# Two layers of a dense network on one core: fewer, larger weight loads, and x transposed in halves

## The chip, the cores and the metric

The kernel runs on one core of a Trainium2 chip. The metric is the device time of one execution in microseconds (us), taken over repeated runs. A profile of one execution gives a span (from the first to the last instruction), which is a little shorter than the device time.

## The reference

The kernel computes a dense layer with a GELU, and a second dense layer, for 512 rows (16 x 32) of 1024 features, with 3584 hidden features; everything is bf16.

```python
B, S, D, F = 16, 32, 1024, 3584
def reference(x, w1, b1, w2, b2):
    h = jnp.einsum("bsd,df->bsf", x, w1) + b1
    h = _gelu(h)
    return jnp.einsum("bsf,fd->bsd", h, w2) + b2
```

x is 1 MB, w1 and w2 are 7 MB each, the output is 1 MB. Each layer is 224 matmuls of 128 x 128 weights against 512 columns.

## The kernel before, in words

Everything is kept in on-chip memory, with a tile of its own for each load (pool `const`), so that no load waits for a buffer. All loads are issued by SyncE (`nc.sync`) in the order in which they are written: the four row tiles of x (`x_sb0` to `x_sb3`, line 60), eight chunks of w1 for its first 512 columns, one for each block `dt` of 128 input features (`w1a`, line 66, 128 KB each), with `b1_rows` (line 70) after the first of them, six chunks of 512 columns over all of `dt` (`w1c`, line 74, 1 MB each), fourteen chunks of w2 (`w2c`, line 83, 512 KB each), and b2. The names in the profile carry a buffer number: w1c_90 is the first 1 MB chunk. A scheduler adds the semaphores; it gives the loads eight semaphores in turn, so that a load is issued only once the load eight places before it has landed.

TensorE first runs `NWARM` = 5 matmuls on zeros (line 99). Then it transposes x: for each row tile, eight 128 x 128 transposes into one PSUM tile (line 109), of which VectorE copies the first half (dt 0 to 3, line 110) and ScalarE the second half (dt 4 to 7, line 111) into `xT`. b1 is transposed and copied after that (lines 114 and 116).

Layer one runs first over a group of `FTC` = 4 output tiles of 128 hidden features together, with `dt` in the outer loop, so that matmuls can start when the first chunk of w1 is there (line 126). Its four GELUs follow (ScalarE, line 121). The remaining 24 tiles run one after the other, each with its eight `dt` matmuls (line 140) and a GELU into `hT`. Layer two runs over two halves of the output columns and four row tiles, with 28 matmuls each (line 154); VectorE adds b2 (line 162) and SyncE stores.

All PSUM tiles come from one pool of eight banks in rotation: the ninth tile waits until the first has been read.

Of the kernel before, what the change touches and what calls it, by code (L numbers as in the profile page):

```python
# [1 line left out]

# [5 lines left out]

ACT = mybir.ActivationFunctionType
ALU = mybir.AluOpType  # L10
FP32 = mybir.dt.float32
BF16 = mybir.dt.bfloat16
PSUM = bass.MemoryType.PSUM

NWARM = 5


@with_exitstack
def kernel(
    ctx: ExitStack,  # L20
    tc: tile.TileContext,
    x: bass.AP,
    w1: bass.AP,
    b1: bass.AP,
    w2: bass.AP,
    b2: bass.AP,
    out: bass.AP,
):
    nc = tc.nc
    P = 128  # L30

    xf = x.flatten_outer_dims()
    of = out.flatten_outer_dims()
    N, D = xf.shape
    F = w1.shape[1]
    assert N % P == 0 and D % P == 0 and F % P == 0
    NT, DT, FT = N // P, D // P, F // P
    assert N <= 512
    FC = 512
    FTC = FC // P  # L40
    assert F % FC == 0
    NFC = F // FC
    DC = 512
    assert D % DC == 0
    NDC = D // DC

    const = ctx.enter_context(tc.tile_pool(name="const", bufs=1))
    opool = ctx.enter_context(tc.tile_pool(name="opool", bufs=3))
    psum = ctx.enter_context(tc.tile_pool(name="psum", bufs=8, space=PSUM))

    def ps_tile(shape, dtype):
        return psum.tile(shape, dtype, name="ps", tag="ps")

    w1v = w1.rearrange("(dt p) f -> p dt f", p=P)
    w2v = w2.rearrange("(ft p) d -> p ft d", p=P)

    x_sb = []
    for nt in range(NT):
        t = const.tile([P, D], BF16, name=f"x_sb{nt}")
        nc.sync.dma_start(t[:], xf[nt * P:(nt + 1) * P, :])  # L60
        x_sb.append(t)

    w1_first = []
    for dt in range(DT):
        t = const.tile([P, FC], BF16, name=f"w1a{dt}")
        nc.sync.dma_start(t[:], w1v[:, dt, 0:FC])  # L66
        w1_first.append(t)
        if dt == 0:
            b1_rows = const.tile([FT, P], BF16, name="b1_rows")
            nc.sync.dma_start(b1_rows[:], b1.rearrange("(ft p) -> ft p", p=P))  # L70
    w1_ch = [None]
    for c in range(1, NFC):
        t = const.tile([P, DT, FC], BF16, name=f"w1c{c}")
        nc.sync.dma_start(t[:], w1v[:, :, c * FC:(c + 1) * FC])
        w1_ch.append(t)

    W2FT = 4
    NW2 = FT // W2FT
    w2_ch = [[None] * NW2 for _ in range(NDC)]
    for dc in range(NDC):  # L80
        for c in range(NW2):
            t = const.tile([P, W2FT, DC], BF16, name=f"w2c{dc}_{c}")
            nc.sync.dma_start(t[:], w2v[:, c * W2FT:(c + 1) * W2FT, dc * DC:(dc + 1) * DC])
            w2_ch[dc][c] = t

    b2_sb = const.tile([P, D], BF16, name="b2_sb")
    nc.sync.dma_start(b2_sb[:], b2[None, :].to_broadcast((P, D)))

    warm = const.tile([P, 1], FP32, name="warm")
    nc.gpsimd.memset(warm[:], 0.0)  # L90
    warm2 = const.tile([P, 1], FP32, name="warm2")
    nc.scalar.activation(warm2[:], warm[:], ACT.Gelu_apprx_tanh)

    zeros = const.tile([P, 512], BF16, name="zeros")
    nc.vector.memset(zeros[:], 0.0)  # L95
    if NWARM:
        warm_ps = ps_tile([P, 512], FP32)
        for i in range(NWARM):
            nc.tensor.matmul(warm_ps[:], lhsT=zeros[:, 0:P], rhs=zeros[:], start=True, stop=True)  # L99

    ident = const.tile([P, P], BF16, name="ident")
    make_identity(nc, ident[:])

    xT = const.tile([P, DT, N], BF16, name="xT")
    H = DT // 2
    for nt in range(NT):
        tp = ps_tile([P, DT, P], BF16)
        for dt in range(DT):
            nc.tensor.transpose(tp[:, dt, :], x_sb[nt][:, dt * P:(dt + 1) * P], ident[:])  # L109
        nc.vector.tensor_copy(xT[:, 0:H, nt * P:(nt + 1) * P], tp[:, 0:H, :])  # L110
        nc.scalar.copy(xT[:, H:DT, nt * P:(nt + 1) * P], tp[:, H:DT, :])  # L111

    b1_ps = ps_tile([P, FT], BF16)
    nc.tensor.transpose(b1_ps[:], b1_rows[:], ident[:FT, :FT])
    b1_sb = const.tile([P, FT], FP32, name="b1_sb")
    nc.vector.tensor_copy(b1_sb[:], b1_ps[:])

    hT = [const.tile([P, N], BF16, name=f"hT{ft}") for ft in range(FT)]

    def gelu(ft, ps):  # L120
        nc.scalar.activation(hT[ft][:], ps[:], ACT.Gelu_apprx_tanh, bias=b1_sb[:, ft:ft + 1], scale=1.0)  # L121

    ps_first = [ps_tile([P, N], FP32) for _ in range(FTC)]
    for dt in range(DT):
        for j in range(FTC):
            nc.tensor.matmul(  # L126
                ps_first[j][:],
                lhsT=w1_first[dt][:, j * P:(j + 1) * P],
                rhs=xT[:, dt, :],
                start=(dt == 0),  # L130
                stop=(dt == DT - 1),
            )
    for j in range(FTC):
        gelu(j, ps_first[j])

    for ft in range(FTC, FT):
        c, j = divmod(ft, FTC)
        ps = ps_tile([P, N], FP32)
        for dt in range(DT):
            nc.tensor.matmul(  # L140
                ps[:],
                lhsT=w1_ch[c][:, dt, j * P:(j + 1) * P],
                rhs=xT[:, dt, :],
                start=(dt == 0),
                stop=(dt == DT - 1),
            )
        gelu(ft, ps)

    for dc in range(NDC):
        for nt in range(NT):  # L150
            ps = ps_tile([P, DC], FP32)
            for ft in range(FT):
                c, j = divmod(ft, W2FT)
                nc.tensor.matmul(  # L154
                    ps[:],
                    lhsT=hT[ft][:, nt * P:(nt + 1) * P],
                    rhs=w2_ch[dc][c][:, j, :],
                    start=(ft == 0),
                    stop=(ft == FT - 1),
                )  # L160
            o_sb = opool.tile([P, DC], BF16, name="o_sb")
            nc.vector.tensor_tensor(o_sb[:], ps[:], b2_sb[:, dc * DC:(dc + 1) * DC], ALU.add)  # L162
            nc.sync.dma_start(of[nt * P:(nt + 1) * P, dc * DC:(dc + 1) * DC], o_sb[:])


# [1 line left out]
_INS = ['x', 'w1', 'b1', 'w2', 'b2']  # L167
_OUTS = [((16, 32, 1024), 'bfloat16')]


# [23 lines left out]
```

## Time and profile before

| what | value |
|---|---|
| device time, median of 6 runs | 110.06 us (109.81 to 111.14) |
| span of the profiled execution | 108.8 us |
| TensorE matmul, busy | 102.1 us (94%), 486 instructions |
| ScalarE / VectorE, busy | 22.7 us / 7.6 us |
| DMA: moved, mean rate | 17.11 MB, 157 GB/s over the span |
| DMA queue of SyncE | 49.0% of 16 engines' span |

Busy time of TensorE is the sum of stretches in which a matmul was under way; matmuls overlap in their pipeline, so their rate is better read from the distance of their starts. A wait is put down to the event that came last before the waiting instruction started. The profile's page also divides the span into 40 slices of 2.72 us, with a digit for the busy share of each engine.

### The profile page before, as it was taken

How to read it: one execution, taken by the hardware profiler on the slowest of the kernel's cores; microseconds unless marked ns; L12 is line 12 of the kernel's file. 1: busy time of each engine (PE TensorE's matmuls, PEld its weight loads, DVE VectorE, ACT ScalarE, POOL GpSimd, SP SyncE). 2: the span in 40 equal slices, each digit the busy share in tenths (PEclk: the TensorE clock that was granted, in tenths of full speed). 3: DMA queues.
4: the chain of work that ended last, by engine and by line, in shares of the span. 5: the costliest groups of instructions: out<-in, count | busy, mean ns of one | idle time of the engine just before them, and what ended most of it. 6: DMA issues, size and time to landing. Idle time of an engine off the chain costs nothing.

```text
span 108.8 us, 1129 instructions
## 1 busy us (share of the span) xinstructions
PE 102.1 (94%) x486; PEld 46.6 (43%) x486; DVE 7.6 (7%) x14; ACT 22.7 (21%) x34; POOL 0.7 (1%) x7
## 2 busy tenths in 40 slices
PE   5869979999999999999999999999999999999970
PEld 2444424444444444444444444444444444444420
DVE  0330000000000000000000020202011020202020
ACT  5160083534435243342522000000000000000000
POOL 2000000000000000000000000000000000000000
PEclk9999999999999999999999999999999999999999
DMA  3998999999999999994000010010101010100101
GB/s 75 277 327 271 366 351 348 352 316 356 333 285 322 364 350 349 351 347 148 4 0 0 0 48 0 5 49 0 48 0 48 0 48 0 44 4 6 48 0 48
DMA packets 16702, 17.11 MB, mean 157 GB/s; under 512 B 698, under 2 KB 16058, under 8 KB 16698
## 3 DMA queue, kind: packets, MB, share of 16 engines
q1 hardware_dynamic: 16698, 17.05, 49.0%
q8 instruction: 4, 0.07, 0.3%
HBM read 16.00 MB, written 1.05 MB: 157 GB/s over the span
## 4 chain that ended last, share of the span: by engine, by line
PE 83%; DMA 11%; SPq 2%; DVE 1%; issue 0%
PE ps L154 44%; PE ps L140 38%; DMA w1c_90<-in_w_dram 7%; DMA w1a_72<-in_w_dram 4%; SPq L60 2%; DVE o_sb L162 1%; SPq L66 0%
## 5 line engine op out<-in xcount | busy, mean ns | idle before, releaser
L162 DVE TENSOR_TENSOR o_sb<-ps,b_sb 128x512 bf16<-128x512 f32 x8 | 5.5, 692 | 92.8 <-PE ps L154 92.8
L140 PE MATMUL ps<-xT,w1c_90 128*128 128x512 bf16 x32 | 7.1, 379 | 0.7 <-DMA w1c_90<-in_w_dram 0.7
L140 PE MATMUL ps<-xT,w1c_92 128*128 128x512 bf16 x32 | 7.1, 379 | 0.0
L140 PE MATMUL ps<-xT,w1c_94 128*128 128x512 bf16 x32 | 7.1, 379 | 0.0
L140 PE MATMUL ps<-xT,w1c_96 128*128 128x512 bf16 x32 | 7.1, 379 | 0.0
L140 PE MATMUL ps<-xT,w1c_98 128*128 128x512 bf16 x32 | 7.1, 379 | 0.0
L140 PE MATMUL ps<-xT,w1c_100 128*128 128x512 bf16 x32 | 7.1, 379 | 0.0
L140 PEld LDWEIGHTS <-w1c_90 128*128 128x128 bf16 x32 | 3.1, 98 | 4.7 <-DMA w1c_90<-in_w_dram 1.1
L140 PEld LDWEIGHTS <-w1c_98 128*128 128x128 bf16 x32 | 3.1, 98 | 3.8
L140 PEld LDWEIGHTS <-w1c_100 128*128 128x128 bf16 x32 | 3.1, 98 | 3.8
L140 PEld LDWEIGHTS <-w1c_96 128*128 128x128 bf16 x32 | 3.1, 98 | 3.8
L140 PEld LDWEIGHTS <-w1c_94 128*128 128x128 bf16 x32 | 3.1, 97 | 3.8
L140 PEld LDWEIGHTS <-w1c_92 128*128 128x128 bf16 x32 | 3.1, 97 | 3.8
L99 PE MATMUL ps<-zeros 128*128 128x512 bf16 x5 | 2.3, 626 | 1.2 <-DVE zeros L95 1.2
L111 ACT COPY xT<-ps 128x512 bf16<-128x512 bf16 x4 | 2.2, 588 | 3.8 <-DVE xT L110 3.8
L110 DVE COPY xT<-ps 128x512 bf16<-128x512 bf16 x4 | 1.7, 425 | 4.8 <-PE ps L109 4.8
L121 ACT ACTIVATE hT_198<-ps,b_sb 128x512 bf16<-128x512 f32 x1 | 0.7, 687 | 5.9 <-PE ps L126 5.9
L154 PE MATMUL ps<-w2c_0_102,hT_198 128*128 128x512 bf16 x4 | 1.5, 379 | 0.0
L154 PE MATMUL ps<-w2c_0_102,hT_199 128*128 128x512 bf16 x4 | 1.5, 379 | 0.0
L154 PE MATMUL ps<-w2c_0_102,hT_200 128*128 128x512 bf16 x4 | 1.5, 379 | 0.0
L154 PE MATMUL ps<-w2c_0_102,hT_201 128*128 128x512 bf16 x4 | 1.5, 379 | 0.0
L154 PE MATMUL ps<-w2c_1_104,hT_202 128*128 128x512 bf16 x4 | 1.5, 379 | 0.0
(144 smaller groups left out, 138.0 us busy)
## 6 DMA issues: line engine op xcount, KB each, us to landing
w1c_90<-in_w_dram SPq DMA_DIRECT2D x1, 1024.0 KB
w1c_92<-in_w_dram SPq DMA_DIRECT2D x1, 1024.0 KB, 10.5
w1c_94<-in_w_dram SPq DMA_DIRECT2D x1, 1024.0 KB, 14.5
w1c_96<-in_w_dram SPq DMA_DIRECT2D x1, 1024.0 KB, 13.1
w1c_98<-in_w_dram SPq DMA_DIRECT2D x1, 1024.0 KB, 13.3
w1c_100<-in_w_dram SPq DMA_DIRECT2D x1, 1024.0 KB, 13.0
out_dram<-o_sb SPq DMA_DIRECT2D x8, 128.0 KB, 1.7
w2c_0_102<-in_w_dram SPq DMA_DIRECT2D x1, 512.0 KB, 9.9
```

The source lines that it names most:

```text
L60: nc.sync.dma_start(t[:], xf[nt * P:(nt + 1) * P, :])
L99: nc.tensor.matmul(warm_ps[:], lhsT=zeros[:, 0:P], rhs=zeros[:], start=True, stop=True)
L110: nc.vector.tensor_copy(xT[:, 0:H, nt * P:(nt + 1) * P], tp[:, 0:H, :])
L111: nc.scalar.copy(xT[:, H:DT, nt * P:(nt + 1) * P], tp[:, H:DT, :])
L121: nc.scalar.activation(hT[ft][:], ps[:], ACT.Gelu_apprx_tanh, bias=b1_sb[:, ft:ft + 1], scale=1.0)
L140: nc.tensor.matmul(ps[:], lhsT=w1_ch[c][:, dt, j * P:(j + 1) * P], rhs=xT[:, dt, :], start=(dt == 0), stop=(dt == DT - 1),)
L154: nc.tensor.matmul(ps[:], lhsT=hT[ft][:, nt * P:(nt + 1) * P], rhs=w2_ch[dc][c][:, j, :], start=(ft == 0), stop=(ft == FT - 1),)
L162: nc.vector.tensor_tensor(o_sb[:], ps[:], b2_sb[:, dc * DC:(dc + 1) * DC], ALU.add)
```

## The change

The change is meant to let layer one start earlier and to have fewer, larger loads. It has these parts:

- The row tiles x1 and x3, and then `b1_rows`, are issued by ScalarE's queue; x0 and x2 by SyncE.
- The first group of layer one has `G0` = 8 tiles of hidden features in place of 4. Its w1 chunks are 128 x 1024 (256 KB); that of dt 0 comes in two halves. Its GELUs are written directly after the last matmul of each tile.
- The rest of w1 comes in two chunks of 1024 columns (2 MB each: w1c8 and w1c16) and one of 512 (w1c24).
- w2 comes in seven chunks of whole rows (1 MB each) in place of fourteen of half rows.
- The warm-up is 22 matmuls of 128 columns in place of 5 of 512.
- x is transposed in half tiles (dt 0 to 3, and dt 4 to 7), each in a PSUM tile of its own: x0 and x1 whole, then b1, then the first halves of x2 and x3, then their second halves. The copies of x2 and x3 are split between the two engines so that the first halves are copied side by side.

```diff
-NWARM = 5
+NWARM = 22
...
-        nc.sync.dma_start(t[:], xf[nt * P:(nt + 1) * P, :])
+        (nc.sync if nt % 2 == 0 else nc.scalar).dma_start(t[:], xf[nt * P:(nt + 1) * P, :])
...
+    b1_rows = const.tile([FT, P], BF16, name="b1_rows")
+    nc.scalar.dma_start(b1_rows[:], b1.rearrange("(ft p) -> ft p", p=P))
...
+    HC = G0C // 2
+    w1p0 = []
+    for h in range(2):
+        t = const.tile([P, HC], BF16, name=f"w1p0_{h}")
+        nc.sync.dma_start(t[:], w1v[:, 0, h * HC:(h + 1) * HC])
+        w1p0.append(t)
+    w1p = [None]
+    for dt in range(1, DT):
+        t = const.tile([P, G0C], BF16, name=f"w1p{dt}")
+        nc.sync.dma_start(t[:], w1v[:, dt, 0:G0C])
+        w1p.append(t)
...
+    while f0 < FT:
+        n = min(8, FT - f0)
+        t = const.tile([P, DT, n * P], BF16, name=f"w1c{f0}")
+        nc.sync.dma_start(t[:], w1v[:, :, f0 * P:(f0 + n) * P])
+        w1_chunks.append((f0, n, t))
+        f0 += n
...
+    for c in range(NW2):
+        t = const.tile([P, W2FT, D], BF16, name=f"w2c{c}")
+        nc.sync.dma_start(t[:], w2v[:, c * W2FT:(c + 1) * W2FT, :])
+        w2_ch.append(t)
...
-            nc.tensor.matmul(warm_ps[:], lhsT=zeros[:, 0:P], rhs=zeros[:], start=True, stop=True)
+            nc.tensor.matmul(warm_ps[:], lhsT=zeros[:], rhs=zeros[:], start=True, stop=True)
...
+    for nt in (0, 1):
+        a = transpose_half(nt, 0)
+        b = transpose_half(nt, 1)
+        copy_half(nt, 0, a, "v")
+        copy_half(nt, 1, b, "s")
+    b1_sb = const.tile([P, FT], FP32, name="b1_sb")
     b1_ps = ps_tile([P, FT], BF16)
     nc.tensor.transpose(b1_ps[:], b1_rows[:], ident[:FT, :FT])
-    b1_sb = const.tile([P, FT], FP32, name="b1_sb")
     nc.vector.tensor_copy(b1_sb[:], b1_ps[:])
+
+    a2 = transpose_half(2, 0)
+    a3 = transpose_half(3, 0)
+    copy_half(2, 0, a2, "s")
+    copy_half(3, 0, a3, "v")
+    b2_ = transpose_half(2, 1)
+    b3_ = transpose_half(3, 1)
+    copy_half(2, 1, b2_, "v")
+    copy_half(3, 1, b3_, "s")
...
-    ps_first = [ps_tile([P, N], FP32) for _ in range(FTC)]
+    ps_first = [ps_tile([P, N], FP32) for _ in range(G0)]
     for dt in range(DT):
-        for j in range(FTC):
+        for j in range(G0):
...
+            if dt == DT - 1:
+                gelu(j, ps_first[j])
```

## The prediction

> **What bounds the kernel now.** I read the page first: TensorE (PE) is busy 94% of the span of 108.8 us, while the DMA engines are busy only in the first half.
>
> ```profile
> PE 102.1 (94%) x486; PEld 46.6 (43%) x486; DVE 7.6 (7%) x14; ACT 22.7 (21%) x34; POOL 0.7 (1%) x7
> ...
> PE   5869979999999999999999999999999999999970
> ...
> DMA  3998999999999999994000010010101010100101
> ```
>
> So the loads end near 50 us, and PE is gapped only in the first six slices and in the last. The chain of waits, in order of time, says the same.
>
> ```profile
> 7.36 7.99 DMA w1c_90<-in_w_dram
> 15.35 0.05 issue
> 15.39 41.61 PE ps L140 x192
> 57.01 48.36 PE ps L154 x224
> ```
>
> From 15.39 on PE runs without a hole, until the last add and store: 41.61 / 192 = 0.217 and 48.36 / 224 = 0.216 us for each matmul. Only what precedes 15.39 can shrink. The timeline of PE in the first 20 us shows that stretch (start, duration, engine, line; in brackets the idle time before it and what ended it).
>
> ```profile
> 1.19 2.31 PE L99 MATMUL ps<-zeros 128*128 128x512 bf16 x5 [1.19 <-DVE zeros L95]
> 3.46 1.00 PE L109 MATMUL ps<-ident,x_sb_64 128*128 128x128 bf16 x8
> ...
> 5.73 0.62 PE L109 MATMUL ps<-ident,x_sb_68 128*128 128x128 bf16 x8 [0.82 <-DMA x_sb_68<-in_x_dram]
> 6.54 0.62 PE L109 MATMUL ps<-ident,x_sb_70 128*128 128x128 bf16 x8 [0.18 <-DMA x_sb_70<-in_x_dram]
> 7.09 0.18 PE L114 MATMUL ps<-ident,b_rows 28*128 28x28 bf16 x1
> 7.67 1.02 PE L126 MATMUL ps<-xT,w1a_72 128*128 128x512 bf16 x4 [0.40 <-DVE xT L110]
> ...
> 13.71 1.03 PE L126 MATMUL ps<-xT,w1a_88 128*128 128x512 bf16 x4
> 15.39 4.92 PE L140 MATMUL ps<-xT,w1c_90 128*128 128x512 bf16 x22 [0.65 <-DMA w1c_90<-in_w_dram]
> ```
>
> There are two losses. The first real matmul starts at 7.67, after the fourth x tile lands (6.53), is transposed and copied. The first 32 matmuls should be over at 13.71 + 4 x 0.216 = 14.57, but the next group starts at 15.39, when w1c_90 has landed: a hole of 0.82 us. Next I read how fast the loads came, by stretches (stretch, length, PE, PEld, DVE, ACT, POOL busy, clock, DMA share, GB/s).
>
> ```profile
> 2.40:3.40 1.00, 1.00 (x3) 0.15 (x1) 0.00 (x0) 0.00 (x0) 0.00 (x0) 1.00 1.03 395
> 3.40:4.60 1.20, 1.20 (x15) 1.14 (x15) 0.10 (x1) 0.00 (x0) 0.00 (x0) 1.00 0.82 157
> 4.60:7.40 2.80, 1.67 (x23) 1.22 (x21) 1.38 (x4) 1.62 (x3) 0.00 (x0) 1.00 1.03 356
> 7.40:9.80 2.40, 2.13 (x10) 0.97 (x10) 0.32 (x2) 0.62 (x2) 0.00 (x0) 1.00 0.83 234
> 9.80:15.35 5.55, 4.94 (x23) 2.05 (x21) 0.00 (x0) 1.22 (x3) 0.00 (x0) 1.00 1.04 356
> 18.35:22.95 4.60, 4.60 (x23) 2.06 (x21) 0.00 (x0) 1.81 (x3) 0.00 (x0) 1.00 1.10 350
> ```
>
> The reader sees two dips: 157 GB/s at 3.4 to 4.6 us, with the engines still 0.82 busy (slow packets, cause not shown), and 234 GB/s at 7.4 to 9.8, where the engines were short of work. In the second, SyncE issues 128 KB chunks and each waits for the transfer eight places earlier to land (w1a_84 is issued at 5.70, x_sb_68 landed at 5.65; w1a_86 at 6.51, when x_sb_70 landed). It costs 2.4 x (350 - 234) = 0.28 MB, 0.8 us of streaming.
>
> **What the Trainium skill says.** "DMA: Bandwidth & Descriptors", section "Issuing engines are not separate DMA queues": issuing from a second engine saves only issue time, as all transfers run on the same 16 engines. In the trace an issue takes 0.42 to 0.43 us on SyncE, and the four x issues go from 0.74 to 2.54. The same page, "Queues, rings and completion order": completion isn't in order over the 16 engines. The trace agrees: w1c_90 is complete when 3.15 MB have been asked for up to its end, but the windows add up to some 4.2 MB moved by then, so the slowest engine lags the mean by about 1 MB. The same page, "Why small descriptors are slow (HBM only)": a packet has a fixed overhead. The trace agrees: 395 GB/s in 2.4 to 3.4 us, when x rows of 2 KB moved, against 350 with w1's 1 KB rows. "TensorE: Matmul & The Clock Gate", section "Part 1: The HAM clock gate": PE is at half clock until it has been busy for about 3.4 us, whatever the number of matmuls. Here matmuls start 0.43 us apart at 1.6 to 2.4 us and 0.216 apart from 7.67; transposes go from 0.10 apart (x_sb_64) to 0.057 (x_sb_66, 4.3 to 4.7), so the clock rose near 4.2, 3.0 us after PE's start.
>
> **The change part by part.**
> *x on two queues.* All x issues end by about 1.6 instead of 2.54, but the data share one set of engines. Earliest: 1.05 MB from 2.4 on at 395 GB/s without the first dip, 2.4 + 2.66 = 5.1, plus the 0.3 by which landing trails: 5.4. Latest: 6.5 as before, as the bytes ahead of the last x byte are the same. I take the middle, 5.95, for x2, x3 and b1_rows, which follows x3 on ScalarE's queue.
> *Transposes and copies in halves.* The b1 transpose now stands on PE ahead of x2 and x3, so all of them wait for b1_rows. After that: b1 0.1, a2 and a3 8 x 0.057 = 0.46, about 0.1 until the output can be read, then DVE's copy of a3, 0.42: 1.1 us to the first matmul. Before it was 7.67 - 6.53 = 1.14. So the interleaving wins next to nothing itself: it replaces four transposes by the b1 pair on the path. ScalarE's copy of a2 (0.59) begins 0.23 earlier than a3's copy and ends with it. The second halves of x2 and x3 are copied beside the first 32 matmuls, which read dt 0 to 3 alone; two of the first eight wait for these copies through the PSUM rotation, but 1.3 and 1.5 us after the first, and the copies are done by then. First matmul: 5.95 + 1.1 = 7.05; bounds 6.5 and 7.65. Win 0.6 (0 to 1.2).
> *ScalarE.* Three issues of about 0.43 go ahead of its table load (1.28) and warm activation (0.20): done at 0.74 + 1.3 + 1.5 = 3.5. Its first copy was at 4.96. Nothing.
> *Warm-up, 22 narrow matmuls for 5 wide.* At half clock 22 x 0.105 (the x_sb_64 spacing) = 2.3 us, against 2.31. Nothing, unless the clock rises later.
> *First group of 8 tiles, in 256 KB chunks.* The first group has 64 matmuls, 13.8 us, so the next chunk is due at 7.05 + 13.8 = 20.9. Each dt chunk lasts PE 8 x 0.216 = 1.73 us and takes 0.26 / 0.35 = 0.75 us to stream, so they keep up. The starvation of 7.4 to 9.8 goes, since twice the bytes are in flight behind the same eight places. Gelus now run as each tile of the group ends: eight in 4.7 us at the 0.58 spacing of before, starting 1.5 us before the group's end; the next PSUM tiles are wanted 1.73 us apart. Hidden.
> *The chunk w1c8.* It is 2 MB and ends at the position, 5.25 MB, at which w1c_94 ended; that landed at 22.95 (issued 8.46, 14.5 us). Less 0.8 for the starvation: 22.2 at the old pace. With 2 KB rows at 395/350 the stretch from about 6.6 shrinks from 15.6 to 13.8: 20.4. So 20.4 to 22.2 against a need at 20.9; I take the early end, since the 395 is in this trace. The hole of 0.82 is gone then.
> *w2 in whole rows.* All seven chunks are now wanted in the first 28 matmuls of layer two, 6 us from about 55 on, rather than over 48 us. Loads ended at 50 before, and don't end later. Hidden. Layer two and the tail keep their matmuls, adds and stores.
> Sum: 0.6 + 0.8 = 1.4 us; 110.06 - 1.4 = 108.7.
>
> **The rivals.** For all: before, the 65th matmul started at 15.39 + 32 x 0.217 = 22.3; the win is 22.3 less its new start.
> (a) *x lands when it did.* Start 7.65, next group at 21.5: 109.3. For: bytes ahead are equal, and the first dip may return. Against: x2 and x3 are asked for 0.5 to 0.9 us sooner.
> (b) *A new hole before w1c8.* The chunk lands at 21.5 to 22.2 and PE waits there, whatever the start: 109.3 to 110.0. For: w1c_94 at 22.95. Against: wider rows.
> (c) *Worse than that.* If the fast engines run ahead by as many packets as before, now of 2 KB, the lag goes from about 1.6 MB at w1c_94 to 3.2: at 395 GB/s (5.25 + 3.2 - 1.3) / 0.395 = 18.1 after 6.6: 24.7, and 112.5. Against: the lag grew with bytes moved, not at once.
> (d) *Cold clock.* If x0 and x1, now loaded side by side, both come near 4.1, PE idles 0.6 between warm-up and transposes, and one more half-clock stretch of 3.4 us may fall on the first 8 matmuls: 8 x 0.21 = 1.7, next group at 22.6, 110.4; two stretches, 112.1.
>
> **How the numbers follow.** The forecast (107.9 to 109.0 with the start's bounds) has 0.53, (a) 0.14, (b) 0.19, (c) 0.06, (d) 0.08. Range 107.9 to 110.5: it leaves out (c), half of (d) and a little below. Faster by over 1% means under 108.96: 0.54. Slower means over 111.16: 0.10. The rest, 0.36, is within.
>
> **What would show it.** Right: first w1p_0 matmul at 6.5 to 7.5; no idle time of PE, or under 0.3 us, put down to w1c8; over 370 GB/s from 8 to 20 us and no dip at 7.4 to 9.8; 0.216 us spacing from the first matmul. Wrong: a wait of over 0.5 us on w1c8 or on a w1p chunk, 0.43 us spacing in the first group, or PE held at the b1 transpose past 6.5.

## The result, and the profile after

| | before | changed |
|---|---|---|
| device time, median | 110.27 us (40 runs) | 109.44 us (20 runs) |
| ratio, changed to before | | 0.9934, 95% interval 0.9912 to 0.9957 |

The changed kernel is faster by 0.7% (0.4 to 0.9% by the interval): 0.83 us between the medians, where 1.36 us was forecast. The profile kept of it is of one of its longer executions (110.90 us), which the ratio leaves out, so a second profile is shown below with the experiments. First the page of the first profile: the busy time of TensorE, its busy tenths in 40 slices, and those of the DMA engines.

```profile
PE 104.1 (95%) x503; PEld 49.7 (46%) x503; DVE 7.5 (7%) x14; ACT 22.1 (20%) x34; POOL 0.7 (1%) x7
...
PE   6799999999999999999999999999999999999970
...
DMA  2999999999999999400000010010101010000101
```

PE now has no slice with a hole from the third on, where before the second to the sixth read 8, 6, 9, 9, 7; and the loads end two slices sooner. The timeline of PE in the same profile (start, duration, engine, line, operation; in brackets the idle time before it):

```profile
0.99 2.53 PE L118 MATMUL ps<-zeros 128*128 128x128 bf16 x22 [0.99 <-DVE zeros L115]
4.10 1.04 PE L130 MATMUL ps<-ident,x_sb_64 128*128 128x128 bf16 x8 [0.58 <-DMA x_sb_64<-in_x_dram]
...
6.01 0.20 PE L147 MATMUL ps<-ident,b_rows 28*128 28x28 bf16 x1
...
7.83 1.91 PE L167 MATMUL ps<-xT,w1p_0_74 128*128 128x512 bf16 x4
9.53 1.22 PE L167 MATMUL ps<-xT,w1p_1_76 128*128 128x512 bf16 x4
10.59 1.89 PE L167 MATMUL ps<-xT,w1p_78 128*128 128x512 bf16 x8
12.31 1.89 PE L167 MATMUL ps<-xT,w1p_80 128*128 128x512 bf16 x8
...
22.67 1.67 PE L180 MATMUL ps<-xT,w1c_92 128*128 128x512 bf16 x7
```

The group of 64 runs into w1c_92 without a wait: that chunk, issued at 7.42, landed 11.7 us later, at 19.1, and is used at 22.67. But the first four matmuls take 1.70 us from 7.83 to 9.53, 0.43 each. The weight loads (PEld) of the same profile show it one by one:

```profile
8.25 0.15 PEld L167 LDWEIGHTS <-w1p_0_74 128*128 128x128 bf16 x1 [0.28 <-issue]
8.68 0.15 PEld L167 LDWEIGHTS <-w1p_0_74 128*128 128x128 bf16 x1 [0.28 <-issue]
9.11 0.15 PEld L167 LDWEIGHTS <-w1p_1_76 128*128 128x128 bf16 x1 [0.28 <-issue]
9.53 0.15 PEld L167 LDWEIGHTS <-w1p_1_76 128*128 128x128 bf16 x1 [0.28 <-issue]
```

They are 0.43 us apart, and from 10.59 to 12.31 eight matmuls take 1.72 us, 0.215 each. So TensorE's clock rose (from half speed to full) at about 9.9, where it rose at about 4.3 in the first profile of before. The column of the granted clock doesn't show it: it reads 1.00 in all stretches, as in these, which give the loads (last column GB/s):

```profile
3.40:4.60 1.20, 0.62 (x7) 0.50 (x6) 0.00 (x0) 0.45 (x2) 0.00 (x0) 1.00 1.04 396
4.60:7.40 2.80, 2.78 (x28) 2.48 (x25) 1.22 (x4) 1.76 (x3) 0.00 (x0) 1.00 1.08 364
7.40:9.80 2.40, 2.40 (x11) 1.18 (x10) 0.67 (x2) 0.59 (x1) 0.00 (x0) 1.00 0.94 326
15.35:22.95 7.60, 7.60 (x37) 3.48 (x36) 0.00 (x0) 1.59 (x3) 0.00 (x0) 1.00 1.05 387
```

Both dips of before, 157 and 234 GB/s, are gone or smaller, and the steady stream is at 387 instead of 350.

### The profile page after: what moved, and what is told of

Same layout as the page of the kernel before. It is cut to its first block, busy times and chain, and to the rows that moved or that the text cites. A ratio compares the mean times of both kernels' runs of the same rounds, so it can differ in the third digit from the quotient of the medians.

```text
span 109.1 us, 1155 instructions
## 1 busy us (share of the span) xinstructions
PE 104.1 (95%) x503; PEld 49.7 (46%) x503; DVE 7.5 (7%) x14; ACT 22.1 (20%) x34; POOL 0.7 (1%) x7
## 4 chain that ended last, share of the span: by engine, by line
PE 93%; DMA 3%; DVE 1%; issue 0%
PE ps L194 44%; PE ps L180 32%; PE ps L167 14%; PE ps L130 3%; DMA x_sb_64<-in_x_dram 3%; DVE o_sb L202 1%; PE ps L147 0%
## 5 line engine op out<-in xcount | busy, mean ns | idle before, releaser
L180 PE MATMUL ps<-xT,w1c_94 128*128 128x512 bf16 x64 | 14.0, 379 | 0.0
L180 PE MATMUL ps<-xT,w1c_92 128*128 128x512 bf16 x64 | 14.0, 379 | 0.0
L180 PEld LDWEIGHTS <-w1c_94 128*128 128x128 bf16 x64 | 6.3, 98 | 7.5
L180 PEld LDWEIGHTS <-w1c_92 128*128 128x128 bf16 x64 | 6.3, 98 | 7.5
L180 PE MATMUL ps<-xT,w1c_96 128*128 128x512 bf16 x32 | 7.1, 379 | 0.0
L180 PEld LDWEIGHTS <-w1c_96 128*128 128x128 bf16 x32 | 3.1, 98 | 3.8
L118 PE MATMUL ps<-zeros 128*128 128x128 bf16 x22 | 2.5, 310 | 1.0 <-DVE zeros L115 1.0
L194 PE MATMUL ps<-w2c_98,hT_201 128*128 128x512 bf16 x8 | 3.0, 379 | 0.0
L194 PE MATMUL ps<-w2c_98,hT_202 128*128 128x512 bf16 x8 | 3.0, 379 | 0.0
L194 PE MATMUL ps<-w2c_98,hT_203 128*128 128x512 bf16 x8 | 3.0, 379 | 0.0
L194 PE MATMUL ps<-w2c_98,hT_204 128*128 128x512 bf16 x8 | 3.0, 379 | 0.0
L194 PE MATMUL ps<-w2c_100,hT_205 128*128 128x512 bf16 x8 | 3.0, 379 | 0.0
L194 PE MATMUL ps<-w2c_100,hT_206 128*128 128x512 bf16 x8 | 3.0, 379 | 0.0
L194 PE MATMUL ps<-w2c_100,hT_207 128*128 128x512 bf16 x8 | 3.0, 379 | 0.0
L194 PE MATMUL ps<-w2c_100,hT_208 128*128 128x512 bf16 x8 | 3.0, 379 | 0.0
L194 PE MATMUL ps<-w2c_102,hT_209 128*128 128x512 bf16 x8 | 3.0, 379 | 0.0
L194 PE MATMUL ps<-w2c_102,hT_210 128*128 128x512 bf16 x8 | 3.0, 379 | 0.0
L194 PE MATMUL ps<-w2c_102,hT_211 128*128 128x512 bf16 x8 | 3.0, 379 | 0.0
L194 PE MATMUL ps<-w2c_102,hT_212 128*128 128x512 bf16 x8 | 3.0, 379 | 0.0
L194 PE MATMUL ps<-w2c_104,hT_213 128*128 128x512 bf16 x8 | 3.0, 379 | 0.0
## 6 DMA issues: line engine op xcount, KB each, us to landing
w1c_92<-in_w_dram SPq DMA_DIRECT2D x1, 2048.0 KB, 11.7
```

Of the source, the lines that this page charges most:

```text
L118: nc.tensor.matmul(warm_ps[:], lhsT=zeros[:], rhs=zeros[:], start=True, stop=True)
L180: nc.tensor.matmul(ps[:], lhsT=w1_rest(dt, ft), rhs=xT[:, dt, :], start=(dt == 0), stop=(dt == DT - 1),)
L194: nc.tensor.matmul(ps[:], lhsT=hT[ft][:, nt * P:(nt + 1) * P], rhs=w2_ch[c][:, j, dc * DC:(dc + 1) * DC], start=(ft == 0), stop=(ft == FT ...
```

## The experiments

Two theories stood against each other at first. **Clock**: the loads behave as forecast, and the missing gain is lost where PE's clock rises late. **Base**: the first profile of before showed an execution longer than most, and part of what I meant to win wasn't there.

**1. The kernel before, a second profile** (no edit).

> The kernel before, once more, for a second profile. Clock theory: the loads and the hole before w1c are as in the first profile (first layer-one matmul at 7.6 to 7.8 us, hole of 0.8 us), and the gain that is missing lies in the changed kernel alone; ratio 1.00. Rival, the base: the first profile of before was a long execution; here the hole before w1c_90 is 0.4 us or less, or the first matmul starts by 7.3, so that the 0.8 us that I counted for the hole was never there to be won in most executions.

Ratio 0.9986 (0.9955 to 1.0016). The timeline of PE:

```profile
7.30 7.07 PE L126 MATMUL ps<-xT,w1a 128*128 128x512 bf16 x32 [0.33 <-DVE xT L110]
14.94 9.24 PE L140 MATMUL ps<-xT,w1c 128*128 128x512 bf16 x42 [0.58 <-DMA w1c<-in_w_dram]
```

The hole is still there (7.30 + 32 x 0.216 = 14.21, then 14.94: 0.73 us), but all of it lies 0.4 us earlier. The base theory is right about the start and the position, and wrong about the hole. The 65th matmul starts at 14.94 + 32 x 0.216 = 21.86, not at 22.3.

**2. The changed kernel, a second profile** (no edit).

> The changed kernel, once more, for a second profile. Clock theory: if the clock has risen before the x2 transposes, the first layer-one matmul starts at 7.0 to 7.2, all matmuls are 0.216 apart and the span is 107.3 to 107.6; if it rises late, as in the first profile (9.9 us), the first starts at 7.8, six are 0.43 apart, and the span is 109.1. Rival: the start is 7.5 or later with a full clock too, because of b1_rows or of the w1p0 chunk. Ratio 0.992 to 0.996 in both.

Ratio 0.9914 (0.9887 to 0.9941), times from 109.03 to 111.03. The timeline of PE:

```profile
4.08 1.26 PE L130 MATMUL ps<-ident,x_sb 128*128 128x128 bf16 x16 [0.56 <-DMA x_sb<-in_x_dram]
5.83 0.18 PE L147 MATMUL ps<-ident,b_rows 28*128 28x28 bf16 x1 [0.50 <-DMA b_rows<-in_b_dram]
5.95 1.07 PE L130 MATMUL ps<-ident,x_sb 128*128 128x128 bf16 x16
7.17 13.97 PE L167 MATMUL ps<-xT,w1p 128*128 128x512 bf16 x64 [0.16 <-DVE xT L136]
20.99 3.19 PE L180 MATMUL ps<-xT,w1c 128*128 128x512 bf16 x14
```

Here the clock has risen early: 64 matmuls in 13.82 us, 0.216 each from the first. The 65th starts at 20.99, against 22.67 in the first profile. The span is 107.4 against 109.1: that is 1.7 us, 0.66 of it before the first layer-one matmul (7.83 - 7.17). Of this, 0.18 is a later b1_rows (6.01 against 5.83); the other 1.5 us are the late clock, since the transposes run at half speed too. PE waits 0.50 us for b1_rows.

**3. The changed kernel with a longer warm-up.**

```diff
-NWARM = 22
+NWARM = 30
```

> Only NWARM is changed, 22 to 30: 8 x 0.105 = 0.84 us more of warm-up, which fills the 0.58 us of idle time of the PE between the warm-up (ends 3.5) and the x0 transposes (4.1). Clock theory: with no idle time the clock rises in the window in which it stayed low before, so the first layer-one matmul starts by 7.2 and the spacing is 0.216 from the first; time 109.1 to 109.4, without times near 110.9: 0.4 us or so less than the changed kernel on average. Rival: the clock's rise is a matter of the free window alone; then the times spread as those of the changed kernel do, 109.1 to 110.9.

Median 109.39 beside 109.72 for the changed kernel on the same chip; times from 109.16 to 109.67. The timeline of PE:

```profile
0.98 3.38 PE L118 MATMUL ps<-zeros 128*128 128x128 bf16 x30 [0.98 <-DVE zeros L115]
4.16 1.63 PE L130 MATMUL ps<-ident,x_sb 128*128 128x128 bf16 x16
...
7.12 13.97 PE L167 MATMUL ps<-xT,w1p 128*128 128x512 bf16 x64 [0.16 <-DVE xT L136]
```

There is no idle time in front of the transposes any more. None of its 11 executions reached 109.7, where 6 of 22 of the changed kernel took 110.67 to 111.03. In the six runs with 30 warm-up matmuls and a first group of 8 (here and below), none of 49 executions took more than 109.80. The clock theory holds for the changed kernel. Filling the pause also makes the warm-up longer, so which of the two removes the long times isn't shown apart.

**4. The first group of 8 and the larger w1 chunks alone, in the kernel before.**

```diff
-    FC = 512
+    G0 = 8
+    G0C = G0 * P
...
-        t = const.tile([P, FC], BF16, name=f"w1a{dt}")
-        nc.sync.dma_start(t[:], w1v[:, dt, 0:FC])
+        t = const.tile([P, G0C], BF16, name=f"w1a{dt}")
+        nc.sync.dma_start(t[:], w1v[:, dt, 0:G0C])
...
+        n = min(8, FT - f0)
+        t = const.tile([P, DT, n * P], BF16, name=f"w1c{f0}")
```

> The kernel before with the first group of 8 tiles, the 256 KB chunks and the 2 MB w1 chunks alone; x, its transposes, the warm-up and w2 stay. By my sum this part is worth the hole, 0.8 us: start at 7.67 as before, no hole before w1c8: ratio 0.992 to 0.993. Rival, the base: the hole is mostly not there in before, ratio 0.996 to 1.00. Second rival: the start is later by 0.1 to 0.3 as w1a0 is now 256 KB.

Ratio 0.9934 (0.9909 to 0.9959), times from 108.86 to 111.57. The timeline of PE:

```profile
7.24 0.18 PE L121 MATMUL ps<-ident,b_rows 28*128 28x28 bf16 x1 [0.28 <-DMA b_rows<-in_b_dram]
7.48 13.97 PE L133 MATMUL ps<-xT,w1a 128*128 128x512 bf16 x64
21.29 2.97 PE L146 MATMUL ps<-xT,w1c 128*128 128x512 bf16 x13
```

The hole is gone. So this part alone gives a gain that can't be told from the whole change's (0.9934 there, 0.9914 in experiment 2). In the profiles the others together start the group 0.31 us sooner (7.17 against 7.48) when the clock is early.

**5. A longer warm-up in the kernel before.**

```diff
-NWARM = 5
+NWARM = 8
```

> The kernel before with NWARM 8 in place of 5: 3 x 0.43 = 1.3 us more of warm-up, to about 4.7 us, into the idle time that PE had between the x1 and the x2 transposes (4.9 to 5.7). Clock theory: the clock's late rise costs the kernel before too; without it the spread ends near 110.3 and the ratio is 0.993 to 0.998. Rival: a late clock belongs to the changed kernel (its idle time at 3.5 to 4.1) and the spread of before comes from its loads; then times still reach 111 and the ratio is 0.998 to 1.002.

Ratio 1.0014 (0.9988 to 1.0041), times from 109.48 to 111.17, as the rival has it. The timeline of PE:

```profile
4.57 2.97 PE L109 MATMUL ps<-ident,x_sb 128*128 128x128 bf16 x32
8.05 7.07 PE L126 MATMUL ps<-xT,w1a 128*128 128x512 bf16 x31 [0.40 <-DVE xT L110]
14.95 9.23 PE L140 MATMUL ps<-xT,w1c 128*128 128x512 bf16 x41
```

The transposes can start only at 4.57, behind the longer warm-up, and they are 0.107 us apart until about 6.7: the clock rose late here too, so the experiment doesn't show what an early clock is worth to the kernel before. Layer one starts at 8.05, 0.75 later than in experiment 1, and the next group starts at 14.95 all the same. It doesn't wait: 8.05 + 32 x 0.216 = 14.96, and in the trace the last piece of the first 1 MB chunk landed at 13.89. So a start that is later by the length of the hole cost nothing here; in the two profiles of the unedited kernel before, the landing of that chunk is what ends the hole.

**6. All of x on one queue again** (with 30 warm-up matmuls).

```diff
-        (nc.sync if nt % 2 == 0 else nc.scalar).dma_start(t[:], xf[nt * P:(nt + 1) * P, :])
+        nc.sync.dma_start(t[:], xf[nt * P:(nt + 1) * P, :])
```

> The changed kernel with 30 warm-up matmuls (as in the third experiment), and all four x tiles on SyncE's queue again; b1_rows stays on ScalarE's and so comes early. If the second queue is what brings x sooner: x3 is there at 6.0 to 6.3 instead of 5.7 or so, and the first layer-one matmul starts at 7.3 to 7.5 instead of 7.12; 109.6 to 109.8. Rival, only issue time is saved and the bytes ahead of x3 are the same: the start stays within 0.15 us of 7.12, 109.3 to 109.5.

Median 109.49, ratio 0.9935 (0.9914 to 0.9955), which can't be told from experiment 3 (0.9911, 0.9881 to 0.9941) by time. In the trace the last x tile comes late; PE's timeline:

```profile
6.77 0.84 PE L130 MATMUL ps<-ident,x_sb 128*128 128x128 bf16 x12 [0.25 <-DMA x_sb<-in_x_dram]
7.78 5.56 PE L167 MATMUL ps<-xT,w1p 128*128 128x512 bf16 x24 [0.16 <-DVE xT L136]
```

and the loads by stretches, beside 396 and 364 GB/s in the changed kernel:

```profile
3.40:4.60 1.20, 1.20 (x15) 1.20 (x13) 0.00 (x0) 0.00 (x0) 0.00 (x0) 1.00 0.97 271
4.60:7.40 2.80, 2.19 (x31) 1.82 (x29) 1.14 (x4) 1.66 (x3) 0.00 (x0) 1.00 0.92 309
```

The start is 0.66 us later than in experiment 3, more than expected, while the median lies where the rival had it (109.3 to 109.5). The profile is of the longest of this kernel's executions (108.87 to 109.80), so the size is uncertain. The direction in the trace agrees with the second queue bringing x sooner; that it saves time isn't shown.

**7. b1 transposed last** (with 30 warm-up matmuls).

```diff
-    b1_ps = ps_tile([P, FT], BF16)
-    nc.tensor.transpose(b1_ps[:], b1_rows[:], ident[:FT, :FT])
-    nc.vector.tensor_copy(b1_sb[:], b1_ps[:])
...
     copy_half(3, 1, b3_, "s")
+    b1_ps = ps_tile([P, FT], BF16)
+    nc.tensor.transpose(b1_ps[:], b1_rows[:], ident[:FT, :FT])
+    nc.vector.tensor_copy(b1_sb[:], b1_ps[:])
```

> The changed kernel with 30 warm-up matmuls, and the b1 transpose and its copy moved behind the second halves of x2 and x3. If b1_rows gates the x2 transposes (they started at 5.89, right behind it): they start at 5.5 to 5.7, and the first matmul at 6.8 to 7.0; the time falls by 0.1 to 0.3 us, 109.1 to 109.3. Rival, x3 lands no sooner than b1_rows: the start moves by less than 0.1 us, only by the pair itself (0.1 to 0.2).

Median 108.73, ratio 0.9889 (0.9857 to 0.9921). The timeline of PE:

```profile
5.38 1.07 PE L130 MATMUL ps<-ident,x_sb 128*128 128x128 bf16 x16 [0.18 <-DMA x_sb<-in_x_dram]
6.38 0.18 PE L155 MATMUL ps<-ident,b_rows 28*128 28x28 bf16 x1
6.61 13.97 PE L166 MATMUL ps<-xT,w1p 128*128 128x512 bf16 x62
```

x2 and x3 are transposed at 5.38, 0.5 us sooner than in experiments 2 and 3, and the start is at 6.61. b1_rows, 7 KB behind two x tiles on its queue, had gated them. The median lies below the 109.1 to 109.3 expected. In this profile the clock rose at about 4.1, sooner than in experiment 3 (about 5.4); experiment 12 shows the same kernel with a later one.

**8. A shorter warm-up in the changed kernel.**

```diff
-NWARM = 22
+NWARM = 10
```

> The changed kernel with NWARM 10 in place of 22: warm-up from 1.0 to 2.1 us, then 2 us idle until x0. Clock theory: the clock then rises late in most executions, with six to fourteen matmuls 0.43 apart in the first group; median 110.6 to 111.2. Rival: the clock's rise depends on the free window alone; median as with 22, 109.4 to 109.7.

Median 110.42, ratio 1.0018 (0.9994 to 1.0042): a little less than I had set, but no execution came below 109.76, and the changed kernel's gain is gone. In its profile all transposes run at half speed and the first matmul starts at 7.78, as in the first profile after; but the clock rose at about 8, so that not six to fourteen matmuls of layer one were slow, only the first.

The next four are experiment 7 with one part changed back, and experiment 7 once more.

**9. w1 loaded and grouped as before.**

```diff
-    G0 = 8
+    G0 = 4
...
-        n = min(8, FT - f0)
+        n = min(4, FT - f0)
```

The chunk of dt 0 is also one load again (those lines are left out).

> The seventh experiment (changed kernel, 30 warm-up matmuls, b1 last) with w1 loaded and grouped as before: a first group of 4 tiles in 128 KB chunks, then 1 MB chunks of 512 columns. If the landing of the first 1 MB chunk is what sets the time of the kernel before, whatever comes ahead of it: the first matmul starts at 6.5 to 6.7, a hole of 1 to 2 us stands before that chunk's group, which starts at 14.4 to 15.0; the ratio is 0.993 to 1.00, and all the earlier start is lost. Rival: the earlier start and the second queue bring the chunk sooner too; group at 13.6 to 14.0, ratio 0.989.

Median 109.99, ratio 0.9958 (0.9932 to 0.9984). The timeline of PE:

```profile
7.24 7.07 PE L157 MATMUL ps<-xT,w1p 128*128 128x512 bf16 x31
14.99 9.24 PE L170 MATMUL ps<-xT,w1c 128*128 128x512 bf16 x41 [0.69 <-DMA w1c<-in_w_dram]
```

The hole is back, and the next group starts at 14.99, within 0.05 us of experiments 1 and 5, though the x loads, the transposes and the warm-up are those of experiment 7. But the start was 7.24, not 6.6 (the clock rose at about 6.2 us here), so this profile has hardly an earlier start that could be lost. It is also of an execution of 110.29 us, longer than the median, and the ratio's interval lies below 1: over all executions the other edits keep a gain of some 0.4% even with the hole.

**10. w1's rest in 1 KB rows.**

```diff
-        n = min(8, FT - f0)
+        n = min(4, FT - f0)
```

> The seventh experiment with the first group of 8 kept, but the rest of w1 in chunks of 512 columns (1 MB, 1 KB rows) in place of 1024. If the group of 8 alone does it: no hole at 20.4, time as in the seventh, 108.6 to 108.9, though the stream at 15 to 23 us falls from 387 to 350 GB/s. Rival: the 2 KB rows are needed; a hole of 0.3 us or more at the end of the group, 109.2 or more.

Median 108.99, ratio 0.9867 (0.9817 to 0.9917). PE's timeline has no hole,

```profile
7.18 13.97 PE L166 MATMUL ps<-xT,w1p 128*128 128x512 bf16 x62 [0.15 <-ACT xT L138]
21.00 3.18 PE L179 MATMUL ps<-xT,w1c 128*128 128x512 bf16 x14
```

though the stream from 15.35 to 22.95 us falls from 387 to 348 GB/s:

```profile
15.35:22.95 7.60, 7.55 (x36) 3.44 (x36) 0.00 (x0) 3.27 (x6) 0.00 (x0) 1.00 1.10 348
```

With chunks of 1 MB the group of 8 hides them without the wider rows, whose speed nothing waits for. A 2 MB chunk in 1 KB rows was not tried.

**11. w2 in fourteen half-row chunks.**

```diff
-        t = const.tile([P, W2FT, D], BF16, name=f"w2c{c}")
-        nc.sync.dma_start(t[:], w2v[:, c * W2FT:(c + 1) * W2FT, :])
+            t = const.tile([P, W2FT, DC], BF16, name=f"w2c{dc}_{c}")
+            nc.sync.dma_start(t[:], w2v[:, c * W2FT:(c + 1) * W2FT, dc * DC:(dc + 1) * DC])
```

> The seventh experiment with w2 in fourteen chunks of half rows as before. Expected to change nothing, as the loads of w2 end long before they are used either way: 108.6 to 108.9, no wait on w2. Rival: 1 KB rows slow the stream enough to show; 109 or more.

Median 108.84, ratio 0.9852 (0.9805 to 0.9899), no wait on w2: no effect of this part is seen.

**12. Experiment 7 once more.**

> The seventh experiment once more, for its interval: ratio 0.986 to 0.991, times 108.6 to 109.0.

Ratio 0.9870 (0.9819 to 0.9922), times from 108.55 to 109.55, four of the six above the 109.0 expected. In its profile the start was 7.26, since the clock was still low for 20 of the 32 transposes: 30 warm-up matmuls keep the clock from costing matmuls of layer one, but not transposes. The changed kernel with 30 warm-up matmuls and b1 last is faster than the kernel before, with medians of 108.73 and 109.24 us. Its ratios (0.9889 and 0.9870) are also below those of the changed kernel (0.9934 and 0.9914), but the intervals overlap.

## Why the prediction was partly wrong

The direction was right, and so was the mechanism of the hole. The size was wrong: 1.36 us forecast, 0.83 measured, and most of what is missing is missing from the earlier start. By the steps:

- *x lands at 5.95, and b1_rows gates the transposes.* Right for b1_rows: the b1 transpose ran at 6.01 and 5.83 in the two profiles. x2 itself was there by 5.38 (experiment 7), so the order of the transposes, which put b1 ahead, took back about half a microsecond.
- *1.1 us from there to the first matmul, at 7.05.* With an early clock 1.34 (5.83 to 7.17), with a late one 1.82.
- *First matmul: "Win 0.6", from 7.67 to 7.05.* **This is the term that failed.** With an early clock the start moved from 7.30 (experiment 1) to 7.17 (experiment 2), by 0.13 us; with a late one it was 7.83, and nothing was won. Of the 0.49 that are missing from 7.67 - 7.05 = 0.62, 0.37 lie in the base: the 7.67 came from one profile, of an execution of 110.71 us where the median was 110.06, and that was in the table. The other 0.12 is the later start after the change.
- *The hole of 0.82 us.* Nearly right: 0.73 in experiment 1.
- *"Before, the 65th matmul started at 15.39 + 32 x 0.217 = 22.3".* The same base: experiment 1 has 21.86, 0.45 us sooner. With this, and the 0.12 for the later end of the group (20.99 against 20.87), the win of an early-clock execution is 21.86 - 20.99 = 0.87 us, or 0.13 + 0.73. These are single profiles; the interval of the ratio is 0.5 to 1.0 us.
- *No hole before w1c8, due at 20.9.* Right. The chunk landed at 19.1 in the first profile, sooner than my 20.4, and the 65th matmul started at 20.99 in the second. In experiment 10 smaller chunks without the wider rows left no hole either.
- *The starvation of 7.4 to 9.8 goes.* Mostly: 326 GB/s in the first profile.
- *Layer two, w2, ScalarE: nothing.* Right as far as tested (experiment 11 for w2; ScalarE's own part was not tried alone).
- *"Sum: 0.6 + 0.8".* The runs do not speak against adding. The hole's removal alone gives a ratio of 0.9934 (experiment 4), all the other edits without it 0.9958 (experiment 9, which has the longer warm-up and b1 last besides); their product is 0.9892, beside 0.9889 and 0.9870 for all of these together (experiments 7 and 12). It is the first of the two terms that was set too large for the change as it was made.
- *Warm-up: "nothing, unless the clock rises later".* This rival, (d), got a chance of 0.08, and 6 of 21 executions, with the profiled one, took 110.6 us or more: its mechanism was right, the chance too small. The idle time that it named (PE waits from 3.5 to 4.1 for x0, which now shares the engines with x1) is there in both profiles. With a warm-up that fills it those times are gone (experiment 3); with one that widens it half of the executions took over 110.4 (experiment 8). A mean over all 20 timed executions is 109.75 against 110.29 before, a gain of 0.5% in place of 0.7%.

The 3.4 us of work that the prediction reckoned with before the clock rises is not what these traces show. In the eleven profiles without that pause the spacing halved 2.8 us (experiment 4, 1.18 to about 4.0) to 5.5 us (experiment 5, 1.18 to about 6.7) after PE's first matmul, always ahead of layer one. With a pause the clock rose at about 4.5 and 9.9 us (0.56 and 0.58 us of pause, the two profiles of the changed kernel) and at about 8 (1.84 us, experiment 8).

The spread of before itself (109.5 to 111.7 in experiment 1) stayed with a longer warm-up (experiment 5), where a start 0.75 us later cost nothing. The traces point to the loads: in the four profiles with the group of 4, 12 of the 16 pieces in which the first 1 MB chunk lands (each has its own event in the trace) were there by 12.71, while the last came at 15.35, 14.90, 13.89 and 14.95 (before, experiments 1, 5 and 9). What delays the last pieces was not tested.

## What to carry to other kernels

Check that the one execution that was profiled is typical of the timed ones before a position in it becomes the base of a difference; here it took 0.65 us longer than the median, and its early stamps were 0.4 us late. Where PE waits for a load before its dense part, find which load ends that wait: an earlier start ahead of it lengthens the wait unless the load comes sooner too, and a larger first group of output tiles hid it here. When such a wait is removed, a late start costs time that the wait had absorbed; in this kernel a warm-up without a pause before the transposes kept the long executions away.

## What the runs showed that I had not expected

- The dip in the loads at 3.4 to 4.6 us came only with x on one queue, though not every time. With all of x on SyncE's queue the rate there was 157, 210, 248, 340 and 271 GB/s (before, experiments 1, 4, 5, 6); with x on two queues it was 396 in both profiles of the changed kernel, and 376 to 403 in the seven others. The Trainium skill, "DMA: Bandwidth & Descriptors", section "Issuing engines are not separate DMA queues", has it that a second issuing engine saves issue time alone; here the rate was higher too. What in the engines causes it was not found.
- With a pause of 0.56 to 0.58 us between warm-up and transposes the clock rose at about 4.5 us in one profile and 9.9 in another, and the column of the granted clock shows 1.00 throughout. The spacing of matmuls shows it.
